# Spectral mixing and SwiGLU feed-forward: another order of loads, weight rounding and idle products in the first batch

## The chip, the cores and the metric

One core of a Trainium2 chip. Its engines run side by side, each through its own queue in order: PE (matrix products, with its weight loads shown as PEld), DVE (vector), ACT (scalar), POOL (GpSimd) and SP, which here only issues DMAs; ACT and POOL issue some too. The metric is the device time of one execution in microseconds (us).

## The reference

Eight sequences of 3008 tokens and 256 channels are filtered in the frequency domain, and the result goes through a SwiGLU block:

```python
X = np.fft.rfft(x, axis=1)                       # x: (8, 3008, 256)
y = np.fft.irfft(X * (filt_r + 1j * filt_i)[None], n=3008, axis=1).astype(np.float32)
t = y.reshape(24064, 256)
g = t @ w_gate                                   # (256, 1536)
silu = g * (1.0 / (1.0 + np.exp(-g)))
out = ((silu * (t @ w_val)) @ w_out).astype(np.float32)
```

The weights of the block come as 64-bit floats; all else is 32-bit.

## The kernel before

**Two halves.** The Fourier transform is done as products with tables, in three stages. Stage 1 multiplies the sequence by a table of 94 rows. Stage 2 has 12 middle steps per batch (`N_TWO`); each takes two of 24 frequency groups through `stage2a` (a product `pb`, then the multiplication by the filter) and `stage2b` (a product `pc`, a copy, and a write `d2` to device memory). Stage 3 reads `d2` back as `t4` and makes, by products `pd`, the sequence `y` in eight blocks. The feed-forward half takes a batch in four chunks (`NCHUNK`) and the hidden units in three groups (`NG`), so a batch has 12 loop steps. It multiplies block matrices with fewer products than the plain way: from the blocks P and Q of the weights, and from sums of them A, B, E for pairs of blocks, come products `wk` (P, Q), `wa` (A, B) and `we` (E). The order of work in a loop step is written out by hand in `SCHEDULE`, 150 tokens: `A01` is the product of that weight, `D01` a difference on POOL that DVE needs for `wa`, `W1` a projection, `t0.1` a slice of the next batch's transform. Each engine executes in that order.

**The first batch** has no batch before it to hide under, so it runs ahead of the loop (lines 869 to 920):

- SP issues the loads in the order of the list `load` (L874): `x` is a quarter of the sequence, `w` a half block of raw weights, `t` a sixth of the stage 2 tables and the filter.
- Stage 1 runs as eight calls of `stage1_first` (L558), each with eight products `wpa` of four columns and two copies, one on ACT and one on DVE. Products of zeros (`idle`, L458) stand before the first call and before calls 4 and 6.
- `turn` (L570) transposes the result for one middle step and copies it on ACT.
- The 12 middle steps follow, with `stage2b` three behind (`lag`, L887). In `stage2a` DVE multiplies out of `pb` into `pt` and `qt` (L600 to L607) and POOL adds them (L609); ACT copies the filter's real part for two steps in three (L616); ACT copies the product `pc` (L627). The write of steps 0 to 7 is issued by SP, that of steps 8 to 11 by ACT.
- Then the reload of `t4`, `preparation.finish(0)`, `warm()` (L464: 14 products of a weight tile, 7 of 188 and 7 of 376 columns), stage 3 for chunk 0 (`wpd` in the profile), three more idle products of zeros, and the sequence sums (L670).

**Preparation** (L377 to L445) rounds the 64-bit weights on the chip. One half block takes DVE operations at L302, L305, L317 and L321, ACT operations at L307, L310, L312 and L314, and products on POOL at L341 and L342 (L329 for the projection weights). `combine_weights` (L351) makes the sums A, B and E for a pair of blocks: one DVE operation for A, an ACT operation at L363 for some pairs, and two POOL operations. All of it is laid out on a line of ticks: half block i starts four ticks after the one before it, the sums of a group of hidden units come from tick 11 of its last half block on. `tick(step, n)` emits the next n ticks into the queues, and POOL's share may be held back until `release`. `finish(step)` emits all that a loop step needs (`need`). In the first batch 2 ticks go into each of the last four calls of stage 1 and into each middle step, the rest into `finish(0)`; from loop step 0 on `TICKS` (20) ticks are spread over a step.

**Loop steps of batch 0.** Chunks 0 to 2 take turns with the three groups of hidden units (steps 0 to 8), so `y` and its sums are written to memory and reloaded. `reload_y` (L925) loads the next step's `y`, 770 KB, by SP; it hangs on the token `A02`, the 81st of 150, in steps 2 to 8. Two buffers of `y` alternate. From step 5 on the next batch's stage 2 loads its tables, filter rows and data with SP as well (`load_two`, L507).

Of the kernel before, what the change touches and what calls it, by code (L numbers as in the profile page):

```python
# [63 lines left out]
NT = 3  # L64
# [3 lines left out]
NB = 7  # L68
# [76 lines left out]
def kernel(  # L145
# [231 lines left out]
    class Preparation:  # L377
# [3 lines left out]
        def __init__(self):  # L381
            self.at, self.held = 0, []

            self.ticks, self.need = {}, {}
            base, ready = [], {}

            def put(t, f, by, pool=False):
                self.ticks.setdefault(t, ([], []))[pool].append(f)
                self.need[by] = max(self.need.get(by, 0), t)

            for i, (_, (use, *at)) in enumerate(weights):
                hid, g = use == "hid", at[0] if use == "hid" else at[0] // JB
                by = ((0, 3, 6) if hid else (1, 4, 7))[g]
                b = base[-1] + (4 if i != 2 * len(BLOCKS) else 8) if i else 0
                if i >= N_EARLY:
                    same = [n for n in range(N_EARLY, i) if spot_of(n) == spot_of(i)]
                    k = 2 if spot_of(i) is None else 1
                    last = base[same[-k]] + 8 if same[k - 1:] else 0
                    b = max(b, last + 8)
                    put(max(last, b - 10), lambda i=i: load_weights(i), by)  # L400
                base.append(b)
                if hid and g == NG - 1:
                    ready.setdefault(NT, b)
                half = []

                def go(half=half, i=i):
                    if not half:
                        half.append(round_half(i))
                    next(half[0], None)

                for n, t in enumerate((0, 1, 2, 3, 4, 6, 7, 9, 10)):
                    put(b + t, go, by, n > 6)
                if hid and at[1:] == [BLOCKS[-1], 1]:
                    for n, pair in enumerate(PAIRS_USED):
                        c = combine_weights(g, *pair)
                        for t in range(3):
                            put(b + 11 + n + t, lambda c=c: next(c, None), by, t == 2)
            self.barriers = sorted((t, step) for step, t in ready.items())
            self.end = max(self.ticks)

# [24 lines left out]
                self.tick(step)  # L445

    preparation = Preparation()
    TICKS = 20

    def bank(name):
        return wps.tile([128, 512], FP32, name=f"w{name}", tag="w")
# [4 lines left out]
    def idle(t, banks, n):  # L458

        for ps in banks:  # L460
            pin(nc.tensor.matmul(out=ps[:, 0:n], lhsT=t[:, 0:128], rhs=t[:, 0:n],
                                 start=True, stop=True))

    def warm():  # L464

        banks = [bank("idle") for _ in range(NB)]
        for n in (TQ, 2 * TQ):
            idle(wt_t[:, 0:2].rearrange("p s z f -> p (s z f)"), banks, n)

    class Spectral:  # L470

# [111 lines left out]
        def stage2a(self, u):  # L583

            if self.b:
                self.load_two(u + 1)
            t2, f = self.t2.pop(u), self.f.pop(u)
            ps = self.bank(f"pb_{self.b}_{u}")
            pt, qt = self.place("p", u), self.place("q", u)
            for i in range(NV):  # L590
                pin(nc.tensor.matmul(out=ps[:, i, :], lhsT=self.tb[u][:, i, 0, :],  # L591
                                     rhs=t2[:, i, :], start=True, stop=True))
            self.p[u] = pt
            yield
            lo, hi = slice(0, 64), slice(64, 128)
            v = nc.vector
            fi = f[hi, 1] if self.b else f[hi]
            if self.b or u in self.real:
                fr = f[:, 0] if self.b else self.real.pop(u)
                pin(v.tensor_tensor(out=pt, in0=ps, in1=fr, op=ALU.mult))  # L600
            else:
                for h in (lo, hi):
                    pin(v.tensor_tensor(out=pt[h], in0=ps[h], in1=f[lo], op=ALU.mult))
            pin(v.scalar_tensor_tensor(out=qt[lo], in0=ps[hi], scalar=-1.0, in1=fi,
                                       op0=ALU.mult, op1=ALU.mult))
            yield
            pin(v.tensor_tensor(out=qt[hi], in0=ps[lo], in1=fi, op=ALU.mult))  # L607
            yield
            pin(add(nc.gpsimd, pt, pt, qt))  # L609

        def real_part(self, u):

# [222 lines left out]
    def run(piece):  # L835
        for _ in piece:
            pass

    with tc.tile_pool(name="start", bufs=1) as spool0:
        x0_t = spool0.tile([128, 8, C], FP32, name="x0")  # L840
        x0.append(x0_t[0:NR])
        tb0 = spool0.tile([128, NS, 2, 128], FP32, name="tb0")
        f0 = spool0.tile([128, NS, C], FP32, name="f0")
        room = spool0.tile([128, 9 * NV, C], FP32, name="room")
        units = [room[:, ts(i, NV)] for i in range(9)] + [x0_t[:, ts(i, NV)] for i in range(4)]
        units += [y_f[:, ts(i, NV * C)].rearrange("p (i c) -> p i c", c=C) for i in range(6)]
        early_places = {"p": (0, 5), "t2": (5, 3), "g": (9, 4), "q": (13, 3), "fr": (16, 3)}
        zero = units[8].rearrange("p i c -> p (i c)")

        one_t = lent[:, 0:2 * NK * 32].rearrange("p (b k) -> p b k", b=2)  # L850
        spare = []
        n = 0
        while n < NPR - 1:
            pair = ORDER[n][0] in "ABE" and ORDER[n + 1][0] in "ABE"
            spare += [n] if pair else []
            n += 2 if pair else 1

        def early(tag, u):
            first, count = early_places[tag]
            return units[first + u % count]  # L860

        def early_raw(i):
            if i >= 8:
                return bits(4 * 7 * 128 + 512 * (i - N_EARLY))
            t = wt_t[:, spare[i]:spare[i] + 2].rearrange("p s z f -> p (s z f)")
            return t.bitcast(U32).rearrange("p (b f two) -> p b f two", b=2, two=2)

        unit_t = spool0.tile([128, 128], FP32, name="unit")
        pin(nc.scalar.dma_start(out=unit_t, in_=unit_dram.ap()))
        pin(nc.vector.memset(zero, 0.0))  # L870
        pin(nc.scalar.activation(out=one, in_=off_t, func=AF.Silu))
        idle(zero, [bank("idle") for _ in range(5)], 512)
        pin(nc.sync.dma_start(out=wf_t, in_=wf_dram.ap()))
        load = [("x", 0), ("x", 1), ("w", 0), ("x", 2), ("w", 1), ("x", 3), ("t", 0), ("w", 2),  # L874
                ("t", 1), ("w", 3), ("t", 2), ("w", 4), ("w", 5), ("t", 3), ("w", 6), ("t", 4),
                ("w", 7), ("t", 5)]
        for what, i in load:
            {"x": spec.load_x, "w": load_weights, "t": spec.load_tables}[what](i)
        for u in range(8):
            if u in (4, 6):  # L880
                idle(zero, [bank("idle") for _ in range(2)], 512)
            spec.stage1_first(u)
            if u > 3:
                preparation.tick(0, 2)
        for u in range(2):
            spec.turn(u)
        lag = 3  # L887
        for u in range(N_TWO + lag):
            if u < N_TWO:
                spec.turn(u + 2)  # L890
                step = spec.stage2a(u)
                next(step)
                next(step)
                preparation.tick(0, 2, hold=True)
                run(step)
                preparation.release()
                spec.real_part(u + 1)
            if u >= lag:
                run(spec.stage2b(u - lag))
            if u == 6:  # L900
                pin(nc.sync.dma_start(out=wi_t, in_=wi_dram.ap()))
                for i in range(8, N_EARLY):
                    load_weights(i)
            if u == N_TWO - 1:
                for i in range(2):
                    spec.load_t4(0, i, 0)
        for i in range(2):
            spec.load_t4(0, i, 1)
        for i in range(2):
            spec.load_t4(1, i)  # L910
        preparation.finish(0)
        warm()
        for step in (0, 2, 1, 3):
            run(spec.stage3(0, step))
        idle(zero, [bank("idle") for _ in range(3)], 512)
        following = Spectral(1)
        for u in range(2):
            following.load_x(u)
# [65 lines left out]
                chore(step, "A23", lambda k, i: cur.load_t4(k, i), step + 2, i)  # L984
    chore(NT, "W2", keep_y, NT)
    for step in range(NT - 1, NT * NG):
        chore(step, "A02", lambda s: reload_y(order_of(0)[s + 1][0], s), step)
    for step in range(NT, NT * NG):
        chore(step, "Q3", lambda s: new_outs(0, *order_of(0)[s]), step)
    for g, step in ((0, 1), (1, 3), (2, 6)):  # L990
# [123 lines left out]
```

## Time and profile before

| | |
|---|---|
| time, median of 4 runs | 2965.55 us (2963.18 to 2966.68) |
| the profiled execution: its time / its span | 2966.68 us / 2964.9 us |
| PE busy | 2925.7 us, 99% of the span |
| weight load, DVE, ACT, POOL busy | 2826.1, 1931.9, 1610.6, 1585.0 us |
| mean granted PE clock | 0.996 of full |
| moved by DMA | 558.59 MB, mean 188 GB/s |

A row of the timeline has the start (us from the span's start), the duration, the engine, the line of the kernel, the operation, what it writes and reads, shapes, and, in brackets, how long its engine stood idle before it and which instruction it waited for. The start and what follows it in the first 90 us, from the windows view (busy us of each engine in the stretch):

| stretch, us | PE | DVE | ACT | POOL | granted clock | DMA share |
|---|---|---|---|---|---|---|
| 10 to 15 | 5.00 | 2.13 | 2.46 | 0.00 | 1.00 | 1.09 |
| 30 to 35 | 3.31 | 4.02 | 2.56 | 1.41 | 1.00 | 1.07 |
| 50 to 60 | 6.35 | 8.71 | 7.39 | 4.66 | 1.00 | 0.70 |
| 60 to 70 | 6.06 | 8.92 | 7.25 | 6.44 | 0.96 | 0.41 |
| 70 to 80 | 8.17 | 4.92 | 4.73 | 6.46 | 0.70 | 0.64 |
| 80 to 90 | 9.96 | 9.27 | 5.89 | 9.12 | 1.00 | 0.60 |

A DMA share near 1 means that the 16 DMA engines have no gap. Idle products count as PE's busy time.

### The profile page before, as it was taken

The numbers are of one execution on the slowest core, as the hardware profiler recorded it, in microseconds if no ns is written. First come the engines' busy times: TensorE is split into PE (matmuls) and PEld (weight loads), VectorE is DVE, ScalarE is ACT, GpSimd is POOL, SyncE is SP. The second block draws the span as 40 slices with busy tenths as digits, with TensorE's granted clock in tenths as the row PEclk, the third lists the DMA queues.
The fourth block names the chain that finished last, engine by engine and source line by source line (L and its number), as shares of the span: only waits on it lengthen the run. The fifth ranks groups of instructions, "written<-read, shape, count | busy, mean of one in ns | idle before, by whom it ended". The sixth has DMA issues, their size and how long they took to land.

```text
span 2964.9 us, 57673 instructions
## 1 busy us (share of the span) xinstructions
PE 2925.7 (99%) x20292; PEld 2826.1 (95%) x20292; DVE 1931.9 (65%) x4379; ACT 1610.6 (54%) x4207; POOL 1585.0 (53%) x1764
## 2 busy tenths in 40 slices
PE   7999999999999999999999999999999999999999
PEld 5888999999999999999999999999999999999999
DVE  5888765576655766557765577656676566766665
ACT  5775455555555555554555554555555555555554
POOL 3776464455545464446554555544564545555453
PEclk9999999999999999999999999999999999999999
DMA  8577865566555655557555566455665565644432
GB/s 212 183 254 257 277 214 165 186 205 199 174 181 184 217 185 174 189 177 223 188 169 183 187 205 209 153 191 187 199 207 161 185 203 189 209 139 148 147 131 89
DMA packets 217081, 558.59 MB, mean 188 GB/s; under 512 B 29872, under 2 KB 107552, under 8 KB 216512
## 3 DMA queue, kind: packets, MB, share of 16 engines
q1 hardware_dynamic: 170954, 485.59, 51.5%
q10 hardware_dynamic: 36912, 45.43, 4.5%
q0 software_dynamic: 8928, 23.89, 2.3%
q8 instruction: 163, 2.67, 0.4%
q14 instruction: 124, 1.02, 0.1%
HBM read 459.73 MB, written 95.05 MB: 187 GB/s over the span
## 4 chain that ended last, share of the span: by engine, by line
PE 92%; DVE 1%; DMA 1%; POOL 1%; issue 0%; ACT 0%; SPq 0%; DVEq 0%; ACTq 0%
PE wa L731 24%; PE wA L810 17%; PE wk L731 16%; PE we L731 12%; PE wG L810 8%; PE wF L810 4%; PE pd L639 3%; PE pa L551 3%; PE pc L623 2%; PE pb L591 2%; DMA y<-y 0%; DMA lent<-de_tbl 0%; DMA d<-lent 0%; POOL wt_t L225 0%; POOL wt_t L228 0%
## 5 line engine op out<-in xcount | busy, mean ns | idle before, releaser
L731 PE MATMUL wa<-y_t,wt_t 128*128 128x188 f32 x4464 | 882.3, 324 | 9.7 <-DVE wa L753 2.8
L731 PEld LDWEIGHTS wa<-y_t,wt_t 128*128 128x128 f32 x4464 | 731.5, 191 | 35.2 <-issue 14.4
L225 POOL TENSOR_TENSOR h<-h 128x376 f32<-128x376 f32 x190 | 182.8, 983 | 793.7 <-DVE h L778 793.7
L810 PE MATMUL wA<-wo_t,h 128*128 128x128 f32 x4608 | 577.9, 275 | 3.8 <-DVE o L225 3.0
L810 PEld LDWEIGHTS wA<-wo_t,h 128*128 128x128 f32 x4608 | 562.8, 192 | 18.1 <-issue 11.2
L731 PE MATMUL wk<-y,wt_t 128*128 128x188 f32 x2976 | 568.1, 324 | 0.1
L228 POOL TENSOR_TENSOR h<-h 128x376 f32<-128x376 f32 x570 | 555.5, 995 | 0.5
L731 PEld LDWEIGHTS wk<-y,wt_t 128*128 128x128 f32 x2976 | 479.1, 191 | 26.3 <-issue 19.8
L228 DVE TENSOR_TENSOR we<-we,m 128x376 f32<-128x376 f32 x576 | 318.7, 556 | 198.4 <-PE we L731 140.9
L731 PE MATMUL we<-y_t,wt_t 128*128 128x188 f32 x2232 | 433.0, 323 | 0.6 <-ACT we L762 0.5
L731 PEld LDWEIGHTS we<-y_t,wt_t 128*128 128x128 f32 x2232 | 370.7, 191 | 1.4 <-ACT we L762 1.0
L228 POOL TENSOR_TENSOR D<-f,f 128x376 f32<-128x376 f32 x288 | 279.9, 985 | 104.7 <-ACT f L746 103.9
L232 DVE SCALAR_TENSOR_TENSOR y<-wk,c 128x376 f32<-128x376 f32 x480 | 245.1, 543 | 132.1 <-ACT we L762 82.5
L766 ACT COPY m<-wa 128x376 f32<-128x376 f32 x576 | 271.9, 472 | 88.4 <-PE wa L731 87.4
L773 ACT ACTIVATE g<-wa 128x188 f32<-128x188 f32 x576 | 187.9, 326 | 189.1 <-PE wa L731 181.6
L810 PE MATMUL wG<-wo_t,h 128*128 128x128 f32 x2304 | 288.3, 275 | 0.6 <-DVE o L225 0.6
L810 PEld LDWEIGHTS wG<-wo_t,h 128*128 128x128 f32 x2304 | 281.4, 192 | 0.8 <-DVE o L225 0.8
L773 ACT ACTIVATE u<-we 128x188 f32<-128x188 f32 x576 | 188.9, 328 | 167.6 <-DVE we L228 148.6
L746 ACT ACTIVATE f<-wk 128x376 f32<-128x376 f32 x288 | 139.2, 483 | 236.3 <-PE wk L731 212.1
L750 ACT COPY c<-wk 128x376 f32<-128x376 f32 x288 | 136.0, 472 | 226.0 <-PE wk L731 226.0
L753 DVE SCALAR_TENSOR_TENSOR x<-wk,f 128x376 f32<-128x376 f32 x192 | 104.6, 545 | 230.3 <-PE wk L731 228.9
L762 ACT COPY we<-y 128x376 f32<-128x376 f32 x480 | 223.8, 486 | 32.7 <-DVE h L778 14.6
(140 smaller groups left out, 3937.6 us busy)
## 6 DMA issues: line engine op xcount, KB each, us to landing
wt_t<-w_all SPq DMA_DIRECT2D x174, 896.0 KB
wt_t<-w_all SPq DMA_DIRECT2D x174, 768.0 KB
t<-d SPq DMA_DIRECT2D x62, 384.0 KB
d<-t ACTq DMA_DIRECT2D x112, 192.0 KB
lent<-de_tbl SPq DMA_DIRECT2D x84, 256.0 KB
lent<-in_filt_r_dram SPq DMA_DIRECT2D x336, 64.0 KB
lent<-d SPq DMA_DIRECT2D x84, 256.0 KB
d<-lent ACTq DMA_DIRECT2D x84, 256.0 KB
```

The lines of the kernel that those rows point to most:

```text
L225: return eng.tensor_tensor(out=dst, in0=a, in1=b, op=ALU.add)
L228: return eng.tensor_tensor(out=dst, in0=a, in1=b, op=ALU.subtract)
L232: return nc.vector.scalar_tensor_tensor(out=dst, in0=a, scalar=-1.0, in1=b, op0=ALU.mult, op1=ALU.subtract)
L551: pin(nc.tensor.matmul(out=ps[0:NK], lhsT=wf_t, rhs=self.x.pop(u), start=True, stop=True))
L731: pin(nc.tensor.matmul(out=ps[:, z], lhsT=self.wt[:, SLOT[p], z], rhs=rhs, start=start and z == 0, stop=True, skip_group_check=True))
L746: pin(act.mul(self.small(f"f{i}", f"f{i}", 1), t[f"k{i}"], -1.0))
L750: pin(act.copy(out=self.small(f"c{i}", f"c{i}", 1), in_=t[f"k{i}"]))
L753: pin(v.scalar_tensor_tensor(out=dst, in0=t[f"k{j}"], scalar=-1.0, in1=t[f"f{i}" if j == 3 else f"D{at}"], op0=ALU.mult, op1=ALU.add))
L762: pin(act.copy(out=self.bank(f"e{at}"), in_=t[f"y{at}"]))
L766: pin(act.copy(out=self.small(f"m{at}", "m", 4), in_=t[f"a{at}"]))
L773: pin(act.activation(out=self.small(op, "g", 3, 1)[:, 0], in_=ps[:, 1], func=AF.Silu))
L810: pin(nc.tensor.matmul(out=self.tiles[at][:, t, :], lhsT=self.hs[i][:, HID[p], t0:t0 + 128], rhs=wo_t[:, JB * q + i, WO[p], :], start=star ...
```

## The change

The loads put the whole sequence first, and each piece of the tables one half block of weights earlier. Stage 1 loses its two pairs of idle products. The ticks in it move to its end: four with the last call and two after the first two turns; middle steps 10 and 11 get none. `stage2b` runs four steps behind instead of three. In middle step 11 of batch 0 the add goes to DVE. One idle product of zeros is put before each of the last two `stage2b`. In place of `warm()` three idle products of 512 columns read the weight slots A13 and Q2, A01 and B13, A02 and A12. On the line of ticks the projection weights of the first group start four ticks later, and the sums of the pairs (2,3) and (0,3) of the first group are due by loop step 1 instead of step 0. `TICKS` is 22. `reload_y` hangs on `P0`, the 28th token, in steps 3 to 8.

```diff
-                b = base[-1] + (4 if i != 2 * len(BLOCKS) else 8) if i else 0
+                b = base[-1] + (4 if i != 2 * len(BLOCKS) else 12) if i else 0
...
-                            put(b + 11 + n + t, lambda c=c: next(c, None), by, t == 2)
+                            put(b + 11 + n + t, lambda c=c: next(c, None),
+                                by if g or n < 4 else 1, t == 2)
...
-    TICKS = 20
+    TICKS = 22
...
-    def warm():
-        banks = [bank("idle") for _ in range(NB)]
-        for n in (TQ, 2 * TQ):
-            idle(wt_t[:, 0:2].rearrange("p s z f -> p (s z f)"), banks, n)
...
-            pin(add(nc.gpsimd, pt, pt, qt))
+            pin(add(nc.vector if self.b == 0 and u == N_TWO - 1 else nc.gpsimd, pt, pt, qt))
...
-        load = [("x", 0), ("x", 1), ("w", 0), ("x", 2), ("w", 1), ("x", 3), ("t", 0), ("w", 2),
-                ("t", 1), ("w", 3), ("t", 2), ("w", 4), ("w", 5), ("t", 3), ("w", 6), ("t", 4),
+        load = [("x", 0), ("x", 1), ("x", 2), ("x", 3), ("w", 0), ("t", 0), ("w", 1), ("t", 1),
+                ("w", 2), ("t", 2), ("w", 3), ("w", 4), ("t", 3), ("w", 5), ("w", 6), ("t", 4),
                 ("w", 7), ("t", 5)]
...
         for u in range(8):
-            if u in (4, 6):
-                idle(zero, [bank("idle") for _ in range(2)], 512)
             spec.stage1_first(u)
-            if u > 3:
-                preparation.tick(0, 2)
+            if u == 7:
+                preparation.tick(0, 4)
         for u in range(2):
             spec.turn(u)
-        lag = 3
+        preparation.tick(0, 2)
+        lag = 4
...
-                preparation.tick(0, 2, hold=True)
+                preparation.tick(0, 2 * (u < N_TWO - 2), hold=True)
...
             if u >= lag:
+                if u - lag >= N_TWO - 2:
+                    idle(zero, [bank("idle")], 512)
                 run(spec.stage2b(u - lag))
...
-        warm()
+
+        for p in ("A13", "A01", "A02"):
+            at = SLOT[p]
+            idle(wt_t[:, at:at + 2].rearrange("p s z f -> p (s z f)"), [bank("idle")], 512)
...
-        chore(step, "A02", lambda s: reload_y(order_of(0)[s + 1][0], s), step)
+        chore(step, "A02" if step < NT else "P0", lambda s: reload_y(order_of(0)[s + 1][0], s), step)
```

## The prediction

> **What bounds the kernel now.** I read the windows view first, cut where PE stops being full:
>
> ```profile
> 85.00:115.00 30.00, 24.82 (x131) 21.73 (x131) 22.43 (x49) 21.25 (x56) 21.07 (x27) 0.89 0.45 143
> 115.00:385.00 270.00, 258.69 (x1734) 244.12 (x1733) 215.71 (x466) 164.87 (x448) 187.98 (x235) 0.99 0.76 256
> 385.00:2900.00 2515.00, 2515.00 (x17654) 2450.47 (x17653) 1600.98 (x3678) 1350.54 (x3538) 1323.30 (x1435) 1.00 0.57 184
> ```
>
> (Stretch, its length, busy time of PE, weight load, DVE, ACT, POOL, granted clock, DMA share, GB/s.) From 385 us on PE has no idle moment, and the change leaves that work alone. Everything must come from the first 385 us: the start (0 to 88 us, before the first product `wk` of the main loop), 5.2 us idle in 85 to 115, 11.3 us in 115 to 385.
>
> The timeline of the start, with the waits in brackets:
>
> ```profile
> 16.09 1.91 PE L461 MATMUL widle<-room 128*128 128x512 f32 x4
> 21.38 1.91 PE L461 MATMUL widle<-room 128*128 128x512 f32 x4
> ...
> 30.15 1.39 DVE L603 TENSOR_TENSOR room<-wpb,f 64x512 f32<-64x512 f32 x2 [1.86 <-PE wpb L591]
> ...
> 71.01 1.26 POOL L225 TENSOR_TENSOR room<-room,y_t 128x512 f32<-128x512 f32 x1 [1.48 <-DVE y_t L607]
> 72.33 2.07 PE L623 MATMUL wpc<-room,tb 128*128 128x256 f32 x4 [1.83 <-POOL room L225]
> 74.44 0.59 ACT L627 COPY x<-wpc 128x512 f32<-128x512 f32 x1 [2.56 <-PE wpc L623]
> 75.92 0.42 DVE L317 SCALAR_TENSOR_TENSOR pw<-wt_t,pw 128x256 uint32<-128x256 uint32 x1 [5.05 <-ACT pw L314]
> ...
> 88.07 0.91 PE L731 MATMUL wk<-y,wt_t 128*128 128x188 f32 x4
> ...
> 96.90 0.97 POOL L228 TENSOR_TENSOR D<-f,f 128x376 f32<-128x376 f32 x1
> 98.52 1.61 PE L731 MATMUL wa<-y_t,wt_t 128*128 128x188 f32 x8 [2.78 <-DVE wa L753]
> ```
>
> The middle steps are DVE's: its first multiply is at 30.15, its last ends at 70.86, 3.4 us a step, DVE busy 8.7 to 8.9 us in 10. Then the last step goes POOL, PE, ACT, and its copy ends at 75.03; I call that T. From T to the first `wk`, 13.0 us, two chains run: the write and reload through memory, and the rest of the weight rounding, which DVE and ACT work off in order. At 96.90 POOL, done late with the sequence sums, delays D01, and PE stands 2.78 us.
>
> **The change part by part.** *First step.* Two idle pairs go. They hold the path from 16.09 to 17.84 and from 21.38 to 23.13: 3.5 us. The sequence must then be there by 8.97 + 7.28 + 3.5 = 19.75 us. The loads (11.6 MB up to the last table) run from 2.3 to about 52 us, 4.3 us a MB; its 3.2 MB end near 16 us. The weights behind it: the first two land near 17 and 23 us and are wanted at 24.2; tables land 5 us or more before use, as before. So this holds.
>
> *Rounding moved.* Six ticks instead of eight precede the middle steps, and three ACT operations (L307, L310, L312: 0.42 + 0.49 + 0.51) now stand in ACT's queue ahead of the first turn copy, behind the last DVE copy of the first step (24.2). Copy at 25.85, product, DVE's multiply at 27.6: of 3.5 us, 2.55 reach DVE.
>
> *Middle steps.* Steps 0 to 9 keep the same DVE operations; the fourth step of lag frees no bank earlier (the bank that `wpc` waits for is still that of two steps before), and PE's waits there are not DVE's: nothing. Step 10 thus starts near 61.5 instead of 63.96. Steps 10 and 11 lose their rounding: 3 x 0.69 = 2.06 each. The last add moves from POOL (1.26, after 0.15) to DVE. No row has a 128x512 add of SBUF operands on DVE; bounds: L600 0.69 (one operand in PSUM), and 1.2 from the 128x256 sums, 0.68 with POOL quiet and 0.95 to 0.99 with POOL busy, that is +0.27 to 0.31 a sum of half the size. I take 0.69, as POOL has only leftovers then. Its end: 61.5 + 4.8 = 66.3, before 72.27. With an idle product (0.95) partly ahead of it, the last `wpc` ends near 67.9 and T moves to about 68.5: 6.5 us sooner. [...]
>
> *What is given back after T.* Skipping four ticks leaves two rounded halves. After the last copy and its DMA issue (0.45) ACT owes seven operations (0.55, 0.55, 0.43, 0.37, 0.55, 0.55, 0.43), not one: T + 3.75. DVE's two follow: T + 4.6, against T + 2.0 (77.00) now. From there the sums, by their spacing of now (225 0.6, 232 0.6, 302 0.5, 225 0.9, 305 0.7, 232 0.9), have A12 at T + 8.8 = 77.3. The three new idle products read A13 with Q2, A01 with B13, A02 with A12, and stand ahead of `wpd` in PE's queue: they hold it for A12, where `warm` ended 81.88 without regard to it. Third idle product at 77.3 to 77.6 plus 0.9 to 1.6: `wpd` at about 79, against 81.72. Its 3.5 us, then the three zero products (2.77): first `wk` at 85.5, 2.5 us sooner. On the other branch DVE's y ends 83.7, POOL's sums (84.4, 7.0 us as from 89.94 to 96.9), the pair (2,3) now behind them (1.5), D01 at 92.9, DVE 0.56: PE's A01 at 94.5 instead of 98.52. **Startup: -4.0.** Bounds: 0, if the gating eats all, and -6.5, if T carries through.
>
> *Clock.* After the 2.78 us wait:
>
> ```profile
> 98.00:100.00 2.00, 1.48 (x8) 1.25 (x8) 2.00 (x6) 0.84 (x3) 2.00 (x3) 0.96 0.98 271
> 100.00:106.00 6.00, 5.09 (x19) 4.99 (x19) 5.12 (x12) 4.72 (x13) 3.12 (x6) 0.50 0.60 193
> ```
>
> PE ran 6 us at half clock, some 2.9 us of its own work lost, but DVE is near full there too, so only about 1.3 (A12 at 105.38, its input ready at 104.1) was on the path. The new wait would be 94.5 - (85.5 + 7.7) = 1.3 us; the nearest row, 1.41 us at 113.59, left the clock at 1.00. **-1.0** (0 to -2.9). [...]
>
> *Ticks in the loop.* 22 for 20, projections four ticks later: both versions reach tick 63 at the end of step 0, then steps 1 and 3 round one half more. POOL is busiest in 145 to 175 (29.69 of 30). Extra 1.4 to 1.7 us of POOL in two steps: PE's waits there are 1.5 us, so 0 to +2; taken 0, as POOL's queue has waited for, not held, PE. The sums of pairs (2,3) and (0,3) come later by design; they are first read in the second half of step 0, over 8 us after.
>
> *Reload of y.* In step 8 it is issued at 359.59 and lands at 367.5:
>
> ```profile
> 359.59 2.26 SPq L927 DMA_DIRECT2D y<-y  x1
> 367.57 0.98 POOL L225 TENSOR_TENSOR y_t<-y 128x376 f32<-128x376 f32 x1 [9.59 <-DMA y<-y]
> 369.08 1.24 PE L731 MATMUL wa<-y_t,wt_t 128*128 128x188 f32 x4 [2.30 <-ACT wa L757]
> 369.00:373.00 4.00, 3.92 (x14) 3.89 (x15) 2.23 (x6) 2.59 (x8) 4.00 (x4) 0.57 0.27 68
> ```
>
> ACT's queue held the copy `wa` behind the sums of the late y. At P0 the issue is some 10 us earlier, ahead of a table load on SP. Gone: 2.3 wait and 4 x 0.43 = 1.7 of slow clock. Given back: 770 KB at 230 GB/s, 3.3 us, ahead of a load for `pb` whose predecessor already cost 0.42 at 350.22; bounds 0 and 3.3, I take 1.0, since both loads together are due before 362.5. **-3.0** (-4.0 to -0.7). Steps 3 to 7: same bytes, PE idle 1.5 at most beside such a load: 0 (-1.5 to +2).
>
> **Sum:** -4.0 - 1.0 - 3.0 = -8.0. The profiled execution took 2966.68 (span 2964.9 and 1.8 around it), 1.1 above the median: 2958.7 there, **2957.6** as a median.
>
> **The rivals.** *The gating eats the startup gain* (0.14). The idle products wait for A12, half clock stretches `wpd`, first `wk` near 88 again; only the reload pays: 2965.5 - 3.0, about 2962. For: the 2.6 us later sums. Against: T is 6.5 us sooner.
> *The early reload is paid for by the table loads* (0.13). Startup only: about 2961. For: the 0.42 us wait and a DMA share of 0.87 in 340 to 360. Against: the same bytes leave the crowded 360 to 369 (1.01).
> *T carries through, clock stays up* (0.07): -6.5 - 2.9 - 4.0, about 2952.
> *Slower* (0.06): in steps 6, 7 and 8 the reload goes in front of a table, filter and t2 load, and PE meets the late `pb` in its queue: 3 x 3.3 = 9.9 lost, no step 8 gain, startup -5.0: about 2970.5. It decides from 5.0 / 3.3, one and a half full reloads. Against it: only one `pb` waited for a DMA in 325 to 385.
> That it does not do what it says is no rival: the changed program's order shows the loads, the idle products and the DVE add where described.
>
> **How the numbers follow.** Main case 0.60; its own range 2953 to 2962. 0.2% is 5.9 us (2959.6), about what a measurement can tell. Faster by more: 0.50 of the main case's 0.60, all of the 0.07, 0.06 of the two middling rivals: 0.63. Slower: 0.05. Within: 0.32. Range 2950.5 to 2964.5: it takes in both middling rivals and the clock case, and leaves out the slower one.
>
> **What would show it.** First step without idle products, ending near 23.4; DVE's first multiply near 27.6; T near 68.5; DVE's A12 near 77; `wpd` near 79, first `wk` near 85.5, the wait for D01 under 1.5 us at clock 1.00; no wait for y near 365. Wrong: a middle step still at 3.4 us in the last two, T after 71, `wpd` after 81, or new `pb` waits for DMA between 270 and 365.

## The result and the profile after

| | before | after |
|---|---|---|
| median of all runs, us | 2964.53 (61 runs, 2961.63 to 2967.87) | 2960.68 (41 runs, 2958.41 to 2962.98) |
| ratio, with 95% interval | | 0.9987 [0.9982, 0.9991] |
| the profiled execution, us / its span | 2966.68 / 2964.9 | 2958.93 / 2956.9 |

The change takes off 3.9 us (2.7 to 5.3 by the interval) where 8.0 were forecast. The time lies in the range, but the gain is half. (The forecast went by a median of 2965.55 us for before; over 61 runs it is 2964.53.) The two profiled executions differ by 7.75 us, close to the forecast, and mislead: that of before lay 2.2 us above its median, that of after 1.8 us below. From here on medians carry the verdicts, and rows serve to find places.

The windows view of after (the columns are those of before's):

```profile
85.00:115.00 30.00, 24.99 (x144) 22.24 (x142) 23.76 (x56) 23.43 (x66) 23.72 (x28) 0.94 0.50 160
115.00:385.00 270.00, 260.37 (x1764) 246.36 (x1765) 213.84 (x471) 165.96 (x448) 191.34 (x241) 1.00 0.78 260
385.00:2900.00 2515.00, 2515.00 (x17659) 2450.68 (x17659) 1599.63 (x3675) 1350.84 (x3538) 1324.61 (x1437) 1.00 0.57 184
```

The last stretch is the same as before. PE's idle time in 115 to 385 fell only from 11.3 to 9.6 us, and that includes a wait for y of 2.30 us that is gone. The window is fixed in time and after runs ahead in it, so this only hints that something new waits in there; the rows below show it.

The timeline of the start in after:

```profile
26.34 1.39 DVE L599 TENSOR_TENSOR room<-wpb,f 64x512 f32<-64x512 f32 x2 [1.53 <-PE wpb L587]
64.59 0.72 DVE L225 TENSOR_TENSOR room<-room,y_t 128x512 f32<-128x512 f32 x1
67.70 0.59 ACT L623 COPY x<-wpc 128x512 f32<-128x512 f32 x1 [1.14 <-PE wpc L619]
70.25 0.42 DVE L317 SCALAR_TENSOR_TENSOR pw<-wt_t,pw 128x256 uint32<-128x256 uint32 x1 [3.88 <-ACT pw L314]
73.89 4.77 PE L463 MATMUL widle<-wt_t 128*128 128x512 f32 x6 [6.23 <-ACT wt_t L363]
78.50 3.71 PE L635 MATMUL wpd<-wi_t,f 96*128 96x94 f32 x32
84.65 0.80 PE L727 MATMUL wk<-y,wt_t 128*128 128x188 f32 x4
92.45 0.97 POOL L228 TENSOR_TENSOR D<-f,f 128x376 f32<-128x376 f32 x1
94.06 2.77 PE L727 MATMUL wa<-y_t,wt_t 128*128 128x188 f32 x8 [1.73 <-DVE wa L749]
```

Every step is there: DVE's first multiply 3.8 us earlier, T at 67.70 + 0.59 = 68.29 (it was 75.03), the idle products held at 73.89 by the weight sums, `wpd` at 78.50, the first `wk` 3.4 us earlier, A01 4.5 us earlier. T is 6.7 us sooner; about half of that reaches `wk`. This is one execution, and an early one: in the second profiles of the two kernels (below) the first `wk` came at 87.64 and 85.65 and A01 at 98.11 and 95.08, so 2.0 and 3.0 us sooner.

In loop step 2 (from about 147 us, by 31 us a step), three waits of PE stand where before had two of about 0.7 us. Before first, then after:

```profile
172.82 0.91 PE L731 MATMUL wa<-y_t,wt_t 128*128 128x188 f32 x4 [0.73 <-ACT m L766]
175.88 0.91 PE L731 MATMUL wa<-y_t,wt_t 128*128 128x188 f32 x4 [0.66 <-ACT m L766]
```

```profile
168.89 0.90 PE L727 MATMUL wa<-y_t,wt_t 128*128 128x188 f32 x4 [1.58 <-ACT m L762]
172.22 0.90 PE L727 MATMUL wa<-y_t,wt_t 128*128 128x188 f32 x4 [0.92 <-ACT m L762]
174.59 0.90 PE L727 MATMUL we<-y_t,wt_t 128*128 128x188 f32 x4 [1.47 <-DVE we L232]
```

After's three sum to 3.97 us. Measured at the transform products that both programs run (`pa`), the lead of after is 5.9 us near 115, 5.3 near 147 and only 2.9 near 183 us. Step 8 then adds about 4 us: SP issues y at 345.59 instead of 359.59, and POOL's first sum of it, at 355.14, waits for a product of PE, not for y:

```profile
345.59 0.34 SPq L927 DMA_DIRECT2D y<-y  x1
355.14 0.98 POOL L225 TENSOR_TENSOR y_t<-y 128x376 f32<-128x376 f32 x1 [0.97 <-PE wa L727]
```

### The profile page after: what moved, and what is told of

Same layout as the page of the kernel before. It is cut to its first block, busy times and chain, and to the rows that moved or that the text cites. A ratio compares the mean times of both kernels' runs of the same rounds, so it can differ in the third digit from the quotient of the medians.

```text
span 2956.9 us, 57617 instructions
## 1 busy us (share of the span) xinstructions
PE 2915.4 (99%) x20266; PEld 2817.0 (95%) x20266; DVE 1926.8 (65%) x4380; ACT 1611.4 (54%) x4207; POOL 1584.2 (54%) x1763
## 4 chain that ended last, share of the span: by engine, by line
PE 93%; DVE 1%; POOL 1%; DMA 1%; ACT 0%; issue 0%; ACTq 0%; DVEq 0%; POOLq 0%
PE wa L727 24%; PE wA L806 17%; PE wk L727 16%; PE we L727 12%; PE wG L806 8%; PE wF L806 4%; PE pd L635 3%; PE pa L547 3%; PE pc L619 2%; PE pb L587 2%; POOL y_t L225 0%; DMA d<-lent 0%; DMA lent<-de_tbl 0%; DVE h L774 0%; DVE y L232 0%
```

## The experiments

There are twelve experiments, two of them repeats of the unchanged kernels. Each time stands beside that of the unchanged kernel before, run beside it on the same chip: 2964.35 us in the first four experiments, 2965.11 in the next four, 2965.07 in the next three, 2964.39 in the last. The interval of most ratios reaches about 2.7 us to either side, so a difference of 2 to 3 us between two versions is near the limit of what one pair can show. The questions: does the wait for y in step 8 cost in every execution (Theory B) or only in some (Theory A); and is the start's lead lost in the loop because of the 22 ticks (Theory C), or does the loop take it back whatever the ticks are (rival D).

**The kernel before again, unchanged.**

> The kernel before, unchanged: 1.000, as the yardstick of noise, and a second profile of it. Theory A (the wait for the late y in loop step 8 belongs to some executions only): the second profile may lack the 2.3 us wait and the half clock near 369 us, and its time is then some 3 to 4 us below the first profiled 2966.7. Theory B (the wait is there in every execution): it is there again, 2 to 2.5 us, and the loss lies elsewhere.

2964.64 us, ratio 1.0001 [0.9992, 1.001]. Its timeline in step 8:

```profile
369.84 0.90 PE L731 MATMUL wa<-y_t,wt_t 128*128 128x188 f32 x4 [1.55 <-ACT wa L757]
```

(Start, duration, engine, line, operation, shapes, count, idle time before and its releaser.) The wait of PE behind the late y, at 369.84, is there again, 1.55 us against 2.30 in the first profile.

**The reload of y alone**, put into the kernel before:

```diff
-        chore(step, "A02", lambda s: reload_y(order_of(0)[s + 1][0], s), step)
+        chore(step, "A02" if step < NT else "P0", lambda s: reload_y(order_of(0)[s + 1][0], s), step)
```

> The kernel before with the reload of y moved to P0 alone. Theory B: -3 to -4 us (0.9986 to 0.9990), as the profile pair shows between 362 and 372 us. Theory A: -0.5 to -2 us (0.9993 to 0.9998), because most executions never paid the wait. A rival, the table loads pay for it: 0 to +2 us, with new waits of pb for DMA between 270 and 365 us.

2961.94 us, ratio 0.9991 [0.9982, 1.0]: 2.4 us less, at the edge of what the interval resolves. There is no wait near 365 to 370. What is given back is a wait for the data of `pb`, 0.82 at 363.15; another, 0.92 at 349.98, is hardly new (0.42 and 0.83 near 350 in the two profiles of before).

**The changed kernel with the reload back at A02** (the same line, the other way):

> The changed kernel with the reload back at A02: the start and the ticks alone. If the start keeps its -4.0 at the first sums and the loop keeps it, 0.9986 to 0.9988. If steps 1 to 3 give back 3 us as the profile pair shows (offset -5.9 at 115 us, -2.9 at 183 us), about 0.9990 to 0.9995 in Theory B; in Theory A, where the reload hardly matters to the median, the same as the changed kernel, 0.9987.

2964.09 us, ratio 0.9997 [0.9988, 1.0006]. Start and ticks without the reload are worth 0.3 us, not measurable. The wait is back, at its largest, though in the slowest execution of this version (2969.36 us):

```profile
370.46 1.62 PE L727 MATMUL wa<-y_t,wt_t 128*128 128x188 f32 x4 [3.40 <-ACT wa L753]
```

**The changed kernel again, unchanged.**

> The changed kernel, unchanged: 0.9987 again on this chip, with a second profile. First wk near 84.7 us, A01 near 94, wpd near 78.5, as these follow from queues on the core; whether the waits of 1.6, 0.9 and 1.5 us at 169, 172 and 175 us recur tells if they belong to the tick change or to one execution.

2960.94 us, ratio 0.9987 [0.9978, 0.9996]; 3.15 us less than the version with the reload back. So Theory B holds in its main point: the reload pays on both sides, 2.4 and 3.15 us. The wait that it removes stands in every profile of a version that issues y late, but not at the 2 to 2.5 us that were expected: 1.55 to 3.40 us so far, and 0.86 and 2.77 in two versions below. The waits of loop step 2 are there in this execution too, 1.58, 0.92 and 1.46 us. This time all engines around the first one can be shown, in order of time:

```profile
168.14 1.07 DVE L302 TENSOR_SCALAR w<-wo_t 128x256 uint32<-128x256 uint32 x1 [1.31 <-POOL lent L225]
169.25 0.42 ACT L307 ACTIVATE w<-w 128x256 f32<-128x256 uint32 x1 [2.05 <-DVE w L302]
169.97 0.46 ACT L762 COPY m<-wa 128x376 f32<-128x376 f32 x1
170.49 0.90 PE L727 MATMUL wa<-y_t,wt_t 128*128 128x188 f32 x4 [1.58 <-ACT m L762]
```

Read from the last line up: PE waits for ACT's copy `m`. That copy's input was there by 168.3, when the last `wa` product before the wait ends, but in ACT's queue it stands behind L307, the conversion of a rounded half block, and that waited 2.05 us for DVE's L302, which itself waited for a sum on POOL. The other two waits have the same look: ACT's L363 and L310 run just ahead of the second `m`, and DVE's L321, 0.94 us long, just ahead of the input of `we`. The rounding of weights is no part of what PE needs here; it sits in the queues ahead of what PE needs. Its operations on DVE are also longer in this stretch than in the start: in the first profile of after 0.86 us on average in 147 to 178, where POOL is busy for 30.72 of 31 us, and 0.35 in 29 to 66, where it is busy for 19.8 of 37. In the kernel before it is 0.73 us in 147 to 178, with POOL at 30.69 us. No run shows that POOL beside them is the cause.

**20 ticks alone changed back:**

```diff
-    TICKS = 22
+    TICKS = 20
```

> The changed kernel with TICKS at 20 alone; the start is untouched (first wk 84.7 to 85.7 us). Theory C: POOL has slack again in loop step 2, the three waits near 170 us shrink from 4.0 us together to 2 or less, time 1 to 2.5 us below the changed kernel, 0.9978 to 0.9984. Rival D: they stay, 0.9987.

2957.33 us (2955.78 to 2959.49), ratio 0.9977 [0.9968, 0.9986], 7.8 us below before and 3.4 below the changed kernel's median. PE's waits over 0.6 us in 115 to 200 are now:

```profile
115.82 2.50 PE L806 MATMUL wF<-wo_t,h 128*128 128x128 f32 x10 [2.38 <-POOL wo_t L329]
...
177.11 0.90 PE L727 MATMUL we<-y_t,wt_t 128*128 128x188 f32 x4 [1.40 <-ACT we L758]
184.51 1.38 PE L806 MATMUL wF<-wo_t,h 128*128 128x128 f32 x10 [1.52 <-DVE h L774]
```

The three waits near 170 are gone. Two others, 1.40 and 1.52, stand a few products behind, where the changed kernel waited 0.54 us and not at all. PE's and POOL's load in that stretch has changed too. The windows view, first the changed kernel again, then this one (columns as before: PE, weight load, DVE, ACT, POOL):

```profile
141.80:181.80 40.00, 34.49 (x234) 31.72 (x235) 34.55 (x75) 27.61 (x77) 39.33 (x52) 1.00 0.60 201
```

```profile
141.80:181.80 40.00, 38.01 (x268) 36.03 (x267) 34.85 (x77) 29.35 (x83) 36.20 (x47) 1.00 0.71 238
```

POOL almost without a gap for 40 us goes with 34.5 us of PE; POOL at 36.2 with 38.0 us. How much of that is gain depends on the cut (3.2 us later, at 145 to 185, it is 34.49 against 36.57 us of PE, with POOL at 36.57 and 36.20). A full POOL is not enough by itself: in 147 to 178 the kernel before has POOL at 30.69 of 31 us and PE at 28.75, the changed kernel 30.72 and 26.01, this one 28.72 and 29.08. And not all of the gain is kept: the new wait at 115.82 belongs to the same preparation, its projection weights coming later when the ticks are wider apart.

Rows place the 3.4 us only in part. The lead over the first profile of before, at `pa` near 115 and near 189 us of before, was 5.89 and 2.87 us in the changed kernel, 3.69 and 1.27 in its second profile, 6.00 and 3.54 here, 6.72 and 5.87, 6.09 and 5.30 in the two versions below that also have 20 ticks and the weight products. So the profile shown here lost as much in this stretch as the changed kernel's second one, the other two lost some 0.8; and by 115 us, before loop step 2, the three with 20 ticks are ahead already.

**All of the tick layout back** (20 ticks, the projection weights after a gap of 8 again, all sums due by step 0):

```diff
-                b = base[-1] + (4 if i != 2 * len(BLOCKS) else 12) if i else 0
+                b = base[-1] + (4 if i != 2 * len(BLOCKS) else 8) if i else 0
...
-                                by if g or n < 4 else 1, t == 2)
+                                by, t == 2)
...
-    TICKS = 22
+    TICKS = 20
```

> The changed kernel with all three edits of the line of ticks undone (20 ticks a step, projections four ticks earlier, all sums of the first group due before the loop). Theory C (the ticks of steps 1 and 2 give back some 2.4 us: POOL is full from 145 to 182 us): those waits fall back to 0.7 and 0.7 us, +1 to +3 us won there; but the burst before the loop is two ticks longer and rounds two projection halves more ahead of y, so the first wk comes 2 to 3 us later. Together within 1.5 us of the changed kernel, 0.9982 to 0.9992 against the kernel before. Rival D (the give-back belongs to the earlier arrival, not to the ticks): waits of 1.6, 0.9 and 1.5 us near 170 us stay.

2958.78 us, ratio 0.998 [0.9971, 0.9989]. More sums now precede the loop, the idle products wait 7.36 us, and the first `wk` comes at 86.80, 2 us later than in after; the waits of loop step 2 are those of before, 0.71 and 0.66 us. By 115 us nothing of the delay is left: the lead over before is 5.18 us there, within the 3.69 to 5.89 of the changed kernel. So the later sums bring `wk` forward, but no time can be put down to them here, and the loop gains.

**Zero products in place of the three that read weights:**

```diff
-        for p in ("A13", "A01", "A02"):
-            at = SLOT[p]
-            idle(wt_t[:, at:at + 2].rearrange("p s z f -> p (s z f)"), [bank("idle")], 512)
+        idle(zero, [bank("idle") for _ in range(NB)], 512)
```

> The changed kernel with the three idle products on the weight tiles replaced by seven products of zeros, which wait for no weight. Gating theory (PE's queue holds wpd for A12): wpd starts near 76 to 77 us, when the reload lands, instead of 78.5 to 79.5; first wk 1.5 to 2.5 us earlier, D01 and A01 1 to 2 us earlier, time 0 to 2 us below the changed kernel, 0.9980 to 0.9987. Rival (ACT's rounding holds the copies of y anyway): wpd earlier, y and A01 not, 0.9987.

2959.19 us, ratio 0.9979 [0.9971, 0.9988]. The timeline of PE:

```profile
76.14 5.25 PE L635 MATMUL wpd<-wi_t,f 96*128 96x94 f32 x32 [1.31 <-DMA f<-d]
81.18 4.68 PE L463 MATMUL widle<-room 128*128 128x512 f32 x6
85.69 0.80 PE L727 MATMUL wk<-y,wt_t 128*128 128x188 f32 x4
...
93.44 1.54 PE L727 MATMUL wa<-y_t,wt_t 128*128 128x188 f32 x8
```

Without the gate `wpd` starts 2.4 us sooner, but now waits for the reloaded data and then runs at a lower clock (0.77 in 76 to 80, 0.50 in 80 to 84), so that `wk` is 1 us later than in after. POOL's sequence sums still start sooner (83.20 against 84.04), and A01 has no wait at all. The gate costs `wk` nothing here: in after the low clock falls on the idle products (0.65 in 73 to 79), without them on `wpd`. Over all executions this version is 1.5 us below the changed kernel, with intervals that overlap.

**The sums of the later groups two ticks apart, and the last pairs of each group due a step later:**

```diff
-                            put(b + 11 + n + t, lambda c=c: next(c, None),
-                                by if g or n < 4 else 1, t == 2)
+                            put(b + 11 + (2 * n if g else n) + t, lambda c=c: next(c, None),
+                                (by if n < 4 else by + 1), t == 2)
```

> The changed kernel with the weight sums of groups 1 and 2 spread over twice as many ticks, the last two pairs due one loop step later (as the first group's already are). If it is the crowd of sums, twelve POOL operations of 0.9 us in some ten us, that fills POOL near 170 us (Theory C, its narrower form), the three waits shrink from 4.0 us to 1.5 or less: 2 to 3 us below the changed kernel, 0.9977 to 0.9982. If POOL is full anyway, the waits move later by some us: 0.9985 to 0.9990.

2962.52 us, ratio 0.9994 [0.9985, 1.0002]: no help, 1.8 us above the changed kernel. The waits near 170 fall to 1.33, 0.61 and 0.81 us, 2.75 together where 1.5 or less was expected, and others come, 1.03 at 179.79 and 1.41 at 202.44. The crowd of these sums is part of those waits, but spreading them moves the loss instead of removing it.

**20 ticks and zero products together:**

> The changed kernel with 20 ticks a step and with zero products in place of the three that read weights. 20 ticks alone gave 2957.3 us, zero products alone 2959.2 against 2960.7 of the changed kernel. If the two act at different places (the waits near 170 us, and POOL's sequence sums ahead of 93 us), the gains add: 2955.5 to 2956.5, ratio near 0.997, A01 near 93.5 us without a wait, no 1.5 us waits near 170 to 175. If the earlier start is only waited away in the loop: 2957.3, the same as 20 ticks alone.

2955.16 us (2954.76 to 2957.32), ratio 0.9967 [0.9955, 0.998]: the two add within the noise (six executions), and this is the fastest version seen, 9.9 us below before. Its profiled execution, 2957.02 us, lies near its slowest; in it `wpd` took 7.11 us at half clock and `wk` came only at 87.23, but A01 at 94.93 without a wait. Waits of 1.40 and 1.51 us stand at 175.96 and 183.35, as with 20 ticks alone; none was expected.

**Start alone:** the changed kernel with 20 ticks and with the reload back at A02:

> The changed kernel with 20 ticks a step and the reload of y back at A02 in all steps: what is left of the change is the start and the later sums. Theory (start pays 4 us, ticks cost 2.4 to 3.5, the reload pays 2.4 to 3.2): 2960 to 2961, ratio near 0.9985, first wk near 85.5 us, a wait for y of 1.5 to 3.5 us in step 8. Rival (the start's gain is waited away later whatever the ticks; 20 ticks and the reload carry it all): 2962 or more, within 0.1% of before.

2959.39 us, ratio 0.9981 [0.9973, 0.999]: 5.7 us below before. With the reload it was 2957.33, so the reload adds 2.1. Against the version with 22 ticks and the late reload (0.3 us below before) the 20 ticks are worth about 5 us here, where they were worth 3.4 with the early reload. Rival D falls: with 20 ticks the loop keeps the start's lead. The expected wait for y was only 0.86 us in the profiled execution, as y came 6.5 us after its issue (353.63 to 360.15), against 9.8 us in the kernel with the wait of 3.40.

**The last add of the middle steps back on POOL** (with 20 ticks):

```diff
-            pin(add(nc.vector if self.b == 0 and u == N_TWO - 1 else nc.gpsimd, pt, pt, qt))
+            pin(add(nc.gpsimd, pt, pt, qt))
```

> The changed kernel with 20 ticks a step and the last add of the middle steps back on POOL. Row by row: POOL takes 1.26 us where DVE took 0.72, so the last product starts about 0.6 us later, and the end of its copy is near 68.9 us instead of 68.3. If that time reaches the loop: 2957.9; if the wait for the weights at the three idle products hides it: 2957.3, first wk still near 85.4 us. If the add on DVE costs more than it gains by holding the rounding behind it: 2956.7.

2957.42 us, ratio 0.9975 [0.9965, 0.9985], against 2957.33: no difference. The add takes 1.44 us on POOL, where DVE took 0.72; T is 68.83 there, against 69.00 in the profile of the 20-tick version with the add on DVE; from DVE's first multiply it is 41.95 and 41.96 us. POOL's add ends at 66.68, and the last `wpc` starts at 67.18, behind the idle product that stands ahead of it in PE's queue (66.32): that product hides the longer add.

**22 ticks in the kernel before:**

```diff
-    TICKS = 20
+    TICKS = 22
```

> The kernel before with 22 ticks in a loop step and nothing else changed. If 22 ticks cost by themselves, because they fill POOL in loop step 2: 2.4 to 3.4 us more, 2967.5 to 2968.5, ratio near 1.001, and waits of PE of about 1.5 us appear between 165 and 180 us. If they cost only together with the later sums and the projection weights that start later in the changed kernel: 2964.5 to 2965.5, the waits of before in that stretch.

2962.02 us, ratio 0.999 [0.9981, 0.9999]: 2.4 us faster (0.3 to 5.6 by the interval), where a loss or no change was expected. PE waits in loop step 2 for 1.12 us at 162.66 and 1.22 at 170.10, and at this cut POOL is less full than in the second profile of the kernel before (37.66 us of the same stretch; in 147 to 178 the two are alike, 30.84 and 30.69 of 31 us). The window is cut later than the two above, as this program is behind the changed kernel by some 3 us:

```profile
145.00:185.00 40.00, 36.61 (x253) 34.19 (x253) 35.02 (x73) 27.37 (x76) 35.28 (x45) 1.00 0.68 216
```

So 22 ticks are no loss by themselves. This is what each layout has on the line of ticks in loop step 2, counted in entries; an entry for DVE and ACT issues up to two operations, or a load, an entry for POOL up to four:

| version | ticks in step 2 | entries for DVE, ACT and loads | entries for POOL | waits over 0.6 us near 160 to 185 |
|---|---|---|---|---|
| before (20) | 83 to 99 | 46 | 14 | 0.73, 0.66 |
| before with 22 | 87 to 99 | 38 | 12 | 1.12, 1.22 |
| after (22) | 85 to 103 | 50 | 16 | 1.58, 0.92, 1.47 |
| after with 20 | 83 to 102 | 52 | 16 | 1.40, 1.52 |

The last group of weights may not begin before its step (a barrier in the line of ticks), at tick 100 before and, because of the wider gap, at tick 104 after. With the old gap, 22 ticks a step reach the barrier early and leave step 2 with less; with the new gap the step gets four entries more for DVE and ACT and two more for POOL than before, packed into 19/22 of its length. Spread over the whole step (20 ticks) the same work costs less. The count alone explains nothing: 20 ticks give step 2 more entries than 22 in the changed kernel. Nor does the pace alone: the kernel before with 22 ticks has it too, and gains. That it is pace and amount together, with the shifted start, fits these four rows but is not shown.

Where the 2.4 us of the kernel before with 22 ticks come from isn't settled. Its wait for y in step 8 is still there (2.77 us). In its profile the lead over the first profile of before is 1.92 us near 115 and 2.40 near 183, so most of it is older than loop step 2; but this execution also began 0.8 us sooner (DVE's first multiply at 29.32).

## Why the prediction was off

*Start.* Right in kind and, within the spread of executions, in size. Forecast against after's row: DVE's first multiply 27.6 and 26.34; T 68.5 and 68.29; `wpd` 79 and 78.50; the first `wk` 85.5 and 84.65; A01 94.5 and 94.06. Over the ten profiles with the new start the first multiply lies at 26.28 to 27.49. One sum is off without effect: the seven ACT operations and the issue after T add up to 3.88 us, not 3.75. The lead of T did not reach `wk` whole, as forecast. Start and clock were to give 5.0 us; the start alone, with 20 ticks, gave 5.7 (3.0 to 8.0 by its interval).

*The moved add.* Taken at 0.69 us, measured at 0.72. POOL ran nothing from 64.76 to 66.12 us, so the add had no POOL instruction beside it for most of its time, and how long it takes with one beside it isn't shown. That it moved at all made no difference, not even to T, which wasn't foreseen: the idle product ahead of the last `wpc` covers it.

*Clock.* Only partly right. The wait before A01 shrank to 1.73 us, where 1.3 was forecast, with the clock at 1.00. The clock did not stay up:

```profile
94.00:96.00 2.00, 1.94 (x7) 1.94 (x8) 2.00 (x6) 1.10 (x4) 2.00 (x4) 0.55 1.09 370
96.00:98.00 2.00, 1.72 (x7) 1.25 (x7) 2.00 (x4) 2.00 (x7) 1.45 (x2) 0.59 0.73 227
98.00:100.00 2.00, 2.00 (x17) 2.00 (x16) 2.00 (x6) 1.81 (x6) 0.61 (x1) 1.00 0.00 0
```

It is about 4 us near half clock instead of 6 to 8, and in the second profile again 6 us (0.50 in 96 to 102). No run separates this term's gain from that of the start.

*Reload of y.* Forecast 3.0 us (0.7 to 4.0). Three pairs of kernels give 2.4, 3.15 and 2.1 us. Inside the bounds, and the give-back is seen as short waits of `pb` for its data, 0.70 at 283.69 and 0.59 at 346.59 in after and at most 1.54 us in any version; the two profiles of before have such waits too, 0.42 and 0.83 us.

*Ticks in the loop.* This is the step that failed: "0 to +2; taken 0, as POOL's queue has waited for, not held, PE". Measured: 2957.33 with 20 ticks against 2960.68, so +3.4 us, above the upper bound. Two things were wrong. First, the place: the text saw one more half block in steps 1 and 3 and overlooked step 2, where the barrier's shift from tick 100 to 104 lets four more entries for DVE and ACT and two more for POOL in, in the stretch that the text names as POOL's busiest. Second, the reason: POOL does hold PE, not directly but through DVE's and ACT's queues, as the chain at 168 to 170 us shows (DVE waits 1.31 us for POOL, ACT 2.05 us for DVE, PE 1.58 us for ACT). Rows of before spoke against it already: the wait of 1.41 us at 113.59 was for POOL, and the 2.78 us before A01 were, by the prediction's own account, for a POOL operation. With 20 ticks, so without this cost, 7.8 us were gained where 8.0 were predicted; part of that closeness is balance, the start alone giving 0.7 us more and the reload 0.9 less than forecast. That the ticks cost the time is measured; the way through the queues is seen at these waits, and that it carries all of the cost is not shown.

The rivals "the gating eats the startup gain" and "the early reload is paid for by the table loads" would have given 2962 and 2961. The second comes nearest to the time, but for a wrong reason: the reload paid, and the lead was lost with the ticks of the weight preparation. About half of T's 6.7 us did not reach `wk`, but not by the gate alone: without it `wk` was no sooner (85.69). The slower case found no support: no `pb` waited more than 1.54 us.

What stays open: why 22 ticks help the kernel before, and how the +3.4 us come about from the density of the ticks and the wider gap together. With 20 ticks the wider gap and the later sums cost nothing (2957.33 us with them, 2958.78 without); 22 ticks with the gap of 8 in the changed kernel would tell the rest, and no run has that.

## What to carry to other kernels

Where background work is dealt out to in-order engines, count what each stage gets of it on every engine, barriers included, and look at the stage in which an engine is already full: a wait on that engine can travel through the other queues to a product that needs none of it (here DVE's 1.31 us for POOL, ACT's 2.05 and PE's 1.58, one behind the other). That a queue has only waited so far says little about what happens when it gets more work: here 0 was taken, and 3.4 us measured.

A profiled execution of before above its median and one of after below it can agree with a forecast to 0.3 us and still prove nothing. Split the change into its parts and measure medians: start 5.7, reload 2.1 to 3.2, ticks -3.4 to about -5 us here.

An idle product that waits for data can also take the half-clock time on itself (a wait of 6.23 us in after, then a clock of 0.50 in 74 to 76 us, and `wpd` in 3.71 us); taking it away moved that time into the real products behind it (`wpd` in 5.25 and 7.11 us, at 0.50 in 80 to 82). The first product of the loop then came no earlier (85.69 and 87.23 us against 84.65); the medians still fell by 1.5 us (22 ticks) and 2.2 us (20 ticks), each within the intervals, with A01 no longer waiting.

## What the hardware showed beyond this

The clock after a short wait was not the same from one execution to the next. With the same program up to this point, A01 waited 1.74 us in the changed kernel run again and 1.75 us in the kernel with the reload back. First the former, then the latter:

```profile
98.00:100.00 2.00, 1.87 (x7) 1.90 (x8) 2.00 (x6) 1.66 (x6) 0.47 (x1) 0.50 0.19 51
```

```profile
98.00:100.00 2.00, 1.59 (x13) 1.62 (x13) 2.00 (x6) 2.00 (x7) 0.75 (x2) 1.00 0.34 96
```

One ran at half clock, the other at full, with 7 and 13 products in the same 2 us. A wait of 1.30 us in the 20-tick version was also followed by half clock (0.50 in 96 to 98). After the waits before A01 of 1.30, 1.44, 1.73, 1.74, 2.78 and 2.92 us the clock came down to 0.50 to 0.55; after that of 1.75 us it stayed at 1.00. With the sums spread (1.74 us) and with the reload alone (3.06 us) the mean of 85 to 115 us was 0.89, as in both profiles of before. So the length of the wait does not tell these executions apart, and what made the difference no run here shows.
